# Theta and the mixing over channels in f16 pairs, and the result's addition on GpSimd, in an attention and spectral-mixing kernel

## The chip, the cores and the metric

The kernel runs on one core of a Trainium2 chip. The metric is the device time of one execution in microseconds, the median of several runs. One more execution was recorded by the hardware profiler; all durations below come from it. The engines are TensorE (PE; its weight loads are listed as PEld), VectorE (DVE), ScalarE (ACT), GpSimd (POOL) and SyncE (SP), which here issues the DMAs. L536 is line 536 of the kernel before.

## The reference

Windowed attention (8 batches, 8 heads, 576 positions, heads of 64) gives `x` with 512 channels; then angles, a mixing over positions (tokens), and a mixing over channels:

```python
scores = scale * np.matmul(q, k.transpose(0, 1, 3, 2))
...
scores = np.where(mask, scores + bias[None], -1000000000.0)   # 0 <= rel < 128, slope * -|rel|
attn = np.exp(scores - max); attn = attn / (sum + 1e-09)
x = np.matmul(attn, v)                                        # (8, 576, 512) after the heads are joined
theta = x @ w_theta
zr, zi = x * np.cos(theta), x * np.sin(theta)
y = einsum('ts,bsd->btd', w_tok_r, zr) + einsum('ts,bsd->btd', w_tok_i, zi)
u = x + y
return u + np.maximum(u @ w_ch, 0.0)
```

All inputs but the weights are float32; the weights `w_theta`, `w_tok_r`, `w_tok_i`, `w_ch` arrive as float64 and are turned into float32 values on the chip.

## The kernel before

**Split products.** TensorE multiplies operands of reduced precision, so each product of precise values is made of three: a value is split into a high part and the remainder (`hi`, `lo`), and hi x hi, hi x lo and lo x hi are summed in PSUM. ScalarE writes the high part, VectorE or GpSimd subtracts it from the value for the low one. Two formats are in use. Token mixing (`mix`, L536) and the attention's values (`values`, L424) use float16 pairs; since float16 has a narrow range of exponents, their values are first multiplied by powers of two. Scores (L365), theta (L475) and channel mixing (L557) use pairs in `F32R`, a 32-bit format, with no scaling; the profile lists it as f32. A matmul has a stationary operand of 128 x 128, loaded as weights, and a moving one: 512 columns in theta (the stationary operand is transposed `x`, the moving one `wth`), 288 in token and channel mixing (half of the 576 positions).

**Stages of a batch.** `attend(b + 1)` runs the four pairs of heads of the next batch: scores, biased and exponentiated (`weigh`, L380 and L383), transposed (`flip`, L388, L395, L396), multiplied with the values (L424) and normalised into `x_sb` (`finish`, L430 to L433). Into it is laid the token mixing of batch b: eight groups of 27 matmuls (L536). Each group's sum is scaled back and added to transposed `x` in `xtf` (L541), which is then `u`; ScalarE writes `u_hi` (L543) and GpSimd `u_lo` (L544). Then comes the `turn` of batch b + 1, over five tiles of positions in the order 1, 2, 3, 4, 0 (tile 0 holds only 64 positions, with high and low part in one operand):

- `columns`: four transposes into PSUM (L455); ScalarE copies `x_hi` (L466), VectorE subtracts `x_lo` (L467), ScalarE copies the plain value to `xtf` (L468).
- `products`: 12 theta matmuls (8 for tile 0), L475. The weights of theta carry the factor 1/(2 pi), so theta counts turns.
- `angle`: rounding to whole turns by adding a large constant (`MAGIC`, L489, ScalarE), the remainder (L490, VectorE, which reads theta's PSUM buffer for the last time), its absolute value (L492), cosine and sine (L496, L497, ScalarE), the products with `x` and a scale (L500), and their split (L446 on ScalarE, L447 on GpSimd).

`rotated` lays one of the channel mixing's eight blocks (12 matmuls at L557, then the relu and the addition of `u` in one VectorE instruction, L560, then the store to DRAM, L562) between the tiles of the turn; two blocks come ahead of it, within the attention (`ahead`, `AHEAD`). The last batch has no turn after it: its blocks follow the token mixing.

**Order.** The program is written in an order and with priorities (`urgent`, `MIX`, `CHAN`, `ROTATE`), from which a planner that simulates the time line makes each engine's order of instructions; on the chip each engine takes its instructions in that order. The matmul results of the turn, of both mixings and of the small sums share three PSUM buffers (`ps_m`, tile `mm`), taken in turn.

**Start.** `start` runs the attention of batch 0 while `unpack` brings in the weights: 17 chunks (four of theta, nine of token mixing, then four of channel mixing, `LATE`), each loaded into one of four places, taken apart by VectorE and ScalarE (L149 to L160), multiplied together by GpSimd (L162) and split (`split`, L170). The raw data of the places lie in buffers named `u_hi`, `u_lo` and `xtf`. For token mixing the sum of absolute values of each row gives the row's power of two (`power`, L119). `scales_first` (L279) puts the first batch's scales together after the last chunk: `spread` (L241) brings a maximum over partitions to all of them by a transpose, a small matmul and VectorE instructions. `batch_scale` (L256) makes a batch's scales from the largest values of `v`.

## Time and profile before

| | |
|---|---|
| median of 3 runs | 770.69 us (770.41 to 771.16) |
| the profiled execution | 770.52 us, span 768.7 us |
| TensorE matmul, weight loads | 703.3 us (91% of the span), 579.9 us (75%) |
| VectorE | 570.4 us (74%), 1554 instructions |
| ScalarE | 478.9 us (62%), 948 instructions |
| GpSimd | 215.6 us (28%), 249 instructions |
| channel matmuls (L557) | 3 x 256 of 288 columns |
| theta matmuls (L475) | 160 + 160 + 128 of 512 columns |

The span runs from the first to the last instruction; the profiled execution's own time is longer by what lies around it. The page divides the span into 40 slices of 19.2 us and gives each engine's busy share in tenths. Matmuls are pipelined, so their busy times overlap each other, and a matmul's duration is longer than the distance to the next. In a list of instructions the columns are the start in us, the duration, the engine, the line, the operation, output<-inputs, the shapes and the count; brackets give idle time before it and what ended it. A row of a group gives, behind the bar, busy time and the mean duration in ns, then the idle time ahead of it.

### The profile page before, as it was taken

To read this page: it belongs to the slowest core of one execution; us is meant where nothing else is said; L and a number is where in the kernel's file an instruction comes from. 1 tells how busy PE (TensorE), PEld (TensorE's weight loads), DVE (VectorE), ACT (ScalarE), POOL (GpSimd) and SP (SyncE) were. 2 spreads that over 40 slices of the span, in tenths; PEclk is the share of its full clock that TensorE was granted. 3 is DMA by queue.
4 is the path that set the end of the run, shared out by engine and by line. 5 is a ranking of instruction groups with operands and counts; after the bars stand their busy time and mean duration, and the time that the engine had idled before them with its cause. 6 is when DMAs were issued, how large, how long until landed. Compare 5 with 4: busy or idle time off the path is not lost.

```text
span 768.7 us, 16184 instructions
## 1 busy us (share of the span) xinstructions
PE 703.3 (91%) x6218; PEld 579.9 (75%) x6221; DVE 570.4 (74%) x1554; ACT 478.9 (62%) x948; POOL 215.6 (28%) x249
## 2 busy tenths in 40 slices
PE   3777588999999999989999999999999999999998
PEld 2466476778878887778878887788778887788777
DVE  5999888888579847797579847887579857864722
ACT  3678638856678547774678647774678547844610
POOL 3343524321233105212232204221233105211420
PEclk8678569999999999999999999999999999999999
DMA  7544220312112200321012301321012200100101
GB/s 259 155 154 152 87 65 2 88 46 64 39 55 81 84 32 32 96 55 60 24 55 72 93 32 32 97 68 48 24 55 82 82 32 32 33 2 32 32 1 62
DMA packets 32621, 49.87 MB, mean 65 GB/s; under 512 B 5664, under 2 KB 22048, under 8 KB 32544
## 3 DMA queue, kind: packets, MB, share of 16 engines
q1 hardware_dynamic: 32544, 48.84, 20.8%
q8 instruction: 49, 0.80, 0.4%
q14 instruction: 28, 0.23, 0.1%
HBM read 39.39 MB, written 9.44 MB: 64 GB/s over the span
## 4 chain that ended last, share of the span: by engine, by line
PE 45%; DVE 29%; ACT 15%; DMA 7%; issue 3%; POOL 0%; SPq 0%; DVEq 0%; ACTq 0%; POOLq 0%
PE mm L536 16%; PE mm L557 7%; PE mm L475 6%; DMA vb<-in_vx_dram 5%; PE s_ps L365 5%; PE t_ps L388 5%; PE acc L424 5%; DVE f L490 4%; ACT s_sb L383 3%; DVE g L492 3%; DVE s_sb L380 2%; DVE g L500 2%; ACT f L489 2%; ACT g L496 2%; DVE pt L396 2%
## 5 line engine op out<-in xcount | busy, mean ns | idle before, releaser
L536 PE MATMUL mm<-wtk_hi,z_hi 128*128 128x288 f16 x576 | 161.9, 288 | 6.1 <-DVE f L487 3.6
L536 PE MATMUL mm<-wtk_lo,z_hi 128*128 128x288 f16 x576 | 161.3, 288 | 0.0
L536 PE MATMUL mm<-wtk_hi,z_lo 128*128 128x288 f16 x576 | 158.8, 287 | 0.0
L536 PEld LDWEIGHTS <-z_hi 128*128 128x128 f16 x1152 | 108.9, 98 | 36.3 <-issue 6.7
L383 ACT ACTIVATE s_sb<-s_sb,fixed 128x256 f32<-128x256 f32 (+1 forms) x256 | 102.1, 469 | 16.8 <-DVE fixed L380 16.7
L544 POOL TENSOR_TENSOR u_lo<-xtf,u_hi 128x288 fp32r<-128x288 f32 x64 | 51.8, 816 | 195.1 <-ACT u_hi L543 178.9
L380 DVE CUSTOM_DVE_ANT_0 s_sb<-s_ps,bands 128x256 f32<-128x256 f32 (+1 forms) x256 | 85.1, 383 | 1.3 <-PE s_ps L365 1.3
L396 DVE SCALAR_TENSOR_TENSOR pt<-t_ps,pt 128x512 f16<-128x512 f32 x112 | 75.9, 685 | 10.5 <-ACT pt L395 10.5
L388 PE MATMUL t_ps<-fixed,s_sb 128*128 128x128 f32 x448 | 77.3, 289 | 6.4 <-ACT s_sb L383 2.0
L395 ACT ACTIVATE pt<-t_ps 128x512 f16<-128x512 f32 x112 | 65.2, 588 | 25.0 <-PE t_ps L388 24.4
L447 POOL TENSOR_TENSOR z_lo<-g,z_hi 128x512 f16<-128x512 f32 x32 | 37.7, 1177 | 134.8 <-ACT z_hi L446 134.8
L301 POOL TENSOR_TENSOR kl<-kr,kh 128x576 fp32r<-128x576 f32 x32 | 50.2, 1569 | 64.3 <-ACT kh L300 64.3
L424 PE MATMUL acc<-vh,pt 128*128 128x65 f16 x1008 | 65.7, 195 | 1.9 <-DVE x_sb L433 1.8
L536 PEld LDWEIGHTS <-z_lo 128*128 128x128 f16 x576 | 57.1, 99 | 13.6
L424 PEld LDWEIGHTS <-pt 128*128 128x128 f16 x1512 | 59.8, 98 | 9.8 <-DVE x_sb L433 2.3
L388 PEld LDWEIGHTS t_ps<-fixed,s_sb 128*128 128x128 f32 x448 | 53.6, 148 | 14.5 <-ACT s_sb L383 6.0
L543 ACT CAST u_hi<-xtf 128x288 fp32r<-128x288 f32 x64 | 27.1, 427 | 59.1 <-DVE xtf L541 58.9
L424 PE MATMUL acc<-vl,pt 128*128 128x64 f16 x504 | 56.3, 193 | 0.0
L557 PE MATMUL mm<-u_hi,wch_hi 128*128 128x288 f32 x256 | 53.0, 321 | 1.3 <-DVE xtf L560 1.1
L496 ACT ACTIVATE g<-g,fixed 128x512 f32<-128x512 f32 (+1 forms) x40 | 29.0, 725 | 39.7 <-DVE g L492 39.2
L365 PE MATMUL s_ps<-kh,qh 64*128 64x256 f32 (+1 forms) x256 | 48.9, 344 | 5.1 <-DVE fixed L380 4.5
L475 PE MATMUL mm<-wth_hi,x_hi 128*128 128x512 f32 x160 | 46.0, 409 | 7.9 <-DVE f L490 7.3
(146 smaller groups left out, 1598.4 us busy)
## 6 DMA issues: line engine op xcount, KB each, us to landing
vb<-in_vx_dram SPq DMA_DIRECT2D x16, 650.0 KB, 4.2
kr<-in_kt_dram SPq DMA_DIRECT2D x32, 288.0 KB, 2.9
out_dram<-xtf SPq DMA_DIRECT2D x64, 144.0 KB, 1.8
qr<-in_qt_dram SPq DMA_DIRECT2D x32, 144.0 KB, 2.7
qr<-in_qt_dram SPq DMA_DIRECT2D x32, 128.0 KB, 2.8
xtf<-in_wtok_dram SPq DMA_DIRECT2D x4, 576.0 KB, 5.0
u_hi<-in_wtok_dram SPq DMA_DIRECT2D x3, 576.0 KB, 3.8
u_lo<-in_wtok_dram SPq DMA_DIRECT2D x2, 576.0 KB, 4.4
```

The costliest lines, as they stand in the source:

```text
L301: nc.gpsimd.tensor_tensor(out=kl, in0=kr, in1=kh.bitcast(F32), op=ALU.subtract)
L365: nc.tensor.matmul(ps[:, e, off:off + kn], qm[rows, q0:q0 + qn], km[rows, k0:k0 + kn], start=(j == 0), stop=(j == last))
L380: nc.vector.tensor_tensor_reduce(out=sb, in0=ps, in1=bias, scale=2.0 ** -(2 * self.p % H + 1), scalar=3.0e38, op0=ALU.add, op1=ALU.min, ac ...
L383: self.exp = nc.scalar.activation(sb, sb, AF.Exp, bias=least, scale=-1.0)
L388: nc.tensor.transpose(t_ps[:, 128 * n:128 * n + 128], self.sc[i, e][:, 128 * j:128 * j + 128], ident)
L395: nc.scalar.activation(pt[:, 0], t_ps, AF.Copy, scale=2.0 ** PEXP)
L396: nc.vector.scalar_tensor_tensor(out=pt[:, 1], in0=t_ps, scalar=2.0 ** PEXP, in1=pt[:, 0], op0=ALU.mult, op1=ALU.subtract)
L424: nc.tensor.matmul(av[:, i, :r.shape[-1]], l, r, start=(n == 0), stop=(n == len(prods) - 1))
L475: nc.tensor.matmul(t_ps, a[:, c * 128:c * 128 + 128], w[:, c, :], start=(k == 0 and c == 0), stop=(k == len(prods) - 1 and c == 3))
L536: nc.tensor.matmul(y_ps[:, :HALF], z[:, c, m * 128:m * 128 + 128], w[:, c, cs], start=(k == 0), stop=(k == 26))
L544: nc.gpsimd.tensor_tensor(out=u_lo[:, m, cs], in0=xtf[:, m, cs], in1=u_hi[:, m, cs].bitcast(F32), op=ALU.subtract)
L557: nc.tensor.matmul(o_ps[:, :HALF], w[:, c, e * 128:e * 128 + 128], u[:, c, cs], start=(k == 0), stop=(k == 11))
```

## The change

Theta's and the channel mixing's pairs become float16. All their scales are powers of two: for theta from the largest `v` of the batch and the largest row sum of theta's weights; for the channel mixing from the row sums of its weights and a bound on `u`, for which the column sums of the absolute token weights are formed by 18 matmuls (`absw`). The scales enter as columns of memory: the high part of `x`, the rounding constant, the factors of the sines and the high part of `u` are now ScalarE instructions with such a column as scale or bias. `u_lo` is made by VectorE. The relu scales back on VectorE into a buffer `r`, and `u` is added to it by GpSimd, in the last batch by VectorE. Two of the four raw places get buffers of their own (`stage`). The core of the diff:

```diff
-    wth_hi = const.tile([128, 4, DM], F32R, name="wth_hi")
+    wth_hi = const.tile([128, 4, DM], F16, name="wth_hi")
...  (the same for wth_lo, wch_hi, wch_lo, x_hi, x_lo, u_hi, u_lo)
+            if kind == "theta":
+                nc.gpsimd.tensor_tensor(out=wth_val[:, c, :], in0=val, in1=ex.bitcast(F32), op=ALU.mult)
+                nc.scalar.activation(val, wth_val[:, c, :], AF.Abs, scale=TURN, accum_out=sums[:, c:c + 1])
+                return
             nc.gpsimd.tensor_tensor(out=val, in0=val, in1=ex.bitcast(F32), op=ALU.mult)
...
+            nc.scalar.activation(junk, val, AF.Abs, accum_out=sums[:, 4 + at:5 + at])
+            nc.vector.tensor_scalar(out=sums[:, 4 + at:5 + at], ..., scalar1=2.0 ** -100, scalar2=None, op0=ALU.max)
+            power(rows[:, 1 + at:2 + at], sums[:, 4 + at:5 + at], WEXP)
...
-                nc.scalar.copy(hi[:, c, :], val)
-                nc.gpsimd.tensor_tensor(out=lo[:, c, :], in0=val, in1=hi[:, c, :].bitcast(F32), op=ALU.subtract)
+        def pieces(hi, lo, val, scale):
+            nc.scalar.activation(hi, val, AF.Copy, scale=scale)
+            nc.vector.scalar_tensor_tensor(out=lo, in0=val, scalar=scale, in1=hi, op0=ALU.mult, op1=ALU.subtract)
...
     def scales_first():
...
+        for k in range(2):
+            s_ps = ps_m.tile([128, 512], F32, name="mm")
+            for c in range(9):
+                nc.tensor.matmul(s_ps[:, :HALF], ones..., absw[:, c, k * HALF:k * HALF + HALF], ...)
+            nc.vector.tensor_reduce(out=wide[:, 1 + k:2 + k], in_=s_ps[:, :HALF], ..., op=ALU.max)
...  (some twenty more small VectorE instructions for lim, fac, blim, bfac)
-            nc.scalar.copy(x_hi, x_ps)
-            nc.vector.tensor_tensor(out=x_lo, in0=x_ps, in1=x_hi.bitcast(F32), op=ALU.subtract)
+            nc.scalar.activation(x_hi, x_ps, AF.Copy, scale=xs)
+            nc.vector.scalar_tensor_tensor(out=x_lo, in0=x_ps, scalar=xs, in1=x_hi, op0=ALU.mult, op1=ALU.subtract)
...
-            nc.scalar.activation(r[:n], th, AF.Copy, bias=MAGIC)
+            nc.scalar.activation(r[:n], th, AF.Identity, bias=magic[:n])
...
-                nc.scalar.activation(g[:n], g[:n], AF.Sin, bias=halfpi[:n], scale=-RAD)
-            st["sin"] = nc.scalar.activation(f[:n], f[:n], AF.Sin, scale=-RAD)
+                nc.scalar.activation(g[:n], g[:n], AF.Sin, bias=halfpi[:n], scale=rad[:n])
+            st["sin"] = nc.scalar.activation(f[:n], f[:n], AF.Sin, scale=rad[:n])
...
-                nc.scalar.copy(u_hi[:, m, cs], xtf[:, m, cs])
-                nc.gpsimd.tensor_tensor(out=u_lo[:, m, cs], in0=xtf[:, m, cs], in1=u_hi[:, m, cs].bitcast(F32),
-                                        op=ALU.subtract)
+                us = st["us"][:, m:m + 1]
+                nc.scalar.activation(u_hi[:, m, cs], xtf[:, m, cs], AF.Copy, scale=us)
+                nc.vector.scalar_tensor_tensor(out=u_lo[:, m, cs], in0=xtf[:, m, cs], scalar=us, in1=u_hi[:, m, cs],
+                                               op0=ALU.mult, op1=ALU.subtract)
...
-                nc.vector.scalar_tensor_tensor(out=xtf[:, e, cs], in0=o_ps[:, :HALF], scalar=0.0, in1=xtf[:, e, cs],
-                                               op0=ALU.max, op1=ALU.add)
+                r = rp.tile([128, HALF], F32, name="r")
+                nc.vector.tensor_scalar(out=r, in0=o_ps[:, :HALF], scalar1=st["uback"], scalar2=0.0, op0=ALU.mult,
+                                        op1=ALU.max)
+                (nc.gpsimd if b < B - 1 else nc.vector).tensor_tensor(out=xtf[:, e, cs], in0=r, in1=xtf[:, e, cs],
+                                                                      op=ALU.add)
```

More of the change, by code (lines that the diff above doesn't have):

```diff
@@ L102, in attn_moe_kernel @@
         nc.vector.memset(scales[:, g:g + 1], -0.125 * 2.0 ** (2 * g + 1))
-    wth_hi = const.tile([128, 4, DM], F32R, name="wth_hi")
-    wth_lo = const.tile([128, 4, DM], F32R, name="wth_lo")
-    wch_hi = const.tile([128, 4, DM], F32R, name="wch_hi")
-    wch_lo = const.tile([128, 4, DM], F32R, name="wch_lo")
+    wth_hi = const.tile([128, 4, DM], F16, name="wth_hi")
+    wth_lo = const.tile([128, 4, DM], F16, name="wth_lo")
+    wch_hi = const.tile([128, 4, DM], F16, name="wch_hi")
+    wch_lo = const.tile([128, 4, DM], F16, name="wch_lo")
     wtk_hi = const.tile([128, 9, S], F16, name="wtk_hi")
     wtk_lo = const.tile([128, 9, S], F16, name="wtk_lo")
-    sums, rows, invs, lim = (rings[name].take() for name in ("sum", "row", "inv", "lim"))
+    wth_val = const.tile([128, 4, DM], F32, name="wth_val")
+    absw = const.tile([128, 9, S], BF16, name="absw")
+    sums, rows, invs, back, lim, fac, blim, bfac, wide, rowt = (
+        rings[name].take() for name in ("sum", "row", "inv", "back", "lim", "fac", "blim", "bfac", "wide", "rowt"))
     nc.vector.memset(rebias, -float(916 << 23))
@@ L170, in split @@
[L170 to L184 removed]
+            src, hi, lo, c, w, kind = jobs[k]
@@ new lines, in together, with split @@
+            nc.vector.tensor_scalar(out=sums[:, 4 + at:5 + at], in0=sums[:, 4 + at:5 + at], scalar1=2.0 ** -100,
+                                    scalar2=None, op0=ALU.max)
+            power(rows[:, 1 + at:2 + at], sums[:, 4 + at:5 + at], WEXP)
+        def split(k, t):
+            _, hi, lo, c, w, kind = jobs[k]
+            if kind == "theta":
+                if c < 3:
+                    return
+                nc.vector.tensor_reduce(out=wide[:, :1], in_=sums[:, :4], axis=mybir.AxisListType.X, op=ALU.max)
+                nc.vector.tensor_scalar(out=wide[:, :1], in0=wide[:, :1], scalar1=2.0 ** -100, scalar2=None,
+                                        op0=ALU.max)
+                power(rows[:, :1], wide[:, :1], WEXP)
+                nc.vector.tensor_scalar(out=rowt[:, :1], in0=rows[:, :1], scalar1=TURN, scalar2=None, op0=ALU.mult)
+                for c in range(4):
+                    pieces(hi[:, c, :], lo[:, c, :], wth_val[:, c, :], rowt[:, :1])
+                return
+            at = c if kind == "channel" else 4 + c
+            pieces(hi[:, c, :], lo[:, c, :], words(k, t)[2].bitcast(F32), rows[:, 1 + at:2 + at])
@@ L199, in unpack @@
                 tiles[k] = load(k)
-    JOBS = ([(wth, wth_hi, wth_lo, c, DM, TURN) for c in range(4)]
-            + [(wtok, wtk_hi, wtk_lo, c, S, "row") for c in ORDER])
-    LATE = [(wch, wch_hi, wch_lo, c, DM, None) for c in range(4)]
+    JOBS = ([(wth, wth_hi, wth_lo, c, DM, "theta") for c in range(4)]
+            + [(wtok, wtk_hi, wtk_lo, c, S, "token") for c in ORDER])
+    LATE = [(wch, wch_hi, wch_lo, c, DM, "channel") for c in range(4)]
     def load_pair(p):
@@ L711, in attn_moe_kernel @@
     x_sb = xp.tile([128, NT, DM], F32, name="x_sb")
-    start(x_sb, unpack(JOBS + LATE, ((big, "u_hi"), (big, "u_lo"), (uf, "xtf"), (uf, "xtf"))))
+    start(x_sb, unpack(JOBS + LATE, ((stage, "raw"), (stage, "raw"), (uf, "xtf"), (uf, "xtf"))))
     scales_first()
```

91 lines of the change are left out of this document (49 added, 42 removed).

## The prediction

> **What bounds the kernel now.** I read the page's busy tenths first, then the busy time by stretch, then the order of time on TensorE, then the waits of one stretch.
>
> ```profile
> span 768.7 us, 16184 instructions
> PE   3777588999999999989999999999999999999998
> DVE  5999888888579847797579847887579857864722
> ```
>
> The profiled execution took 770.5 us, 1.8 of them around its span of 768.7; the median of the three runs, 770.69, is 0.2 above it. The sum below is made on 770.5. From the eighth slice (some 135 us) on TensorE is full; before that VectorE is, with nines in slices two to four.
>
> ```profile
> 80.00:98.00 18.00, 8.51 (x46) 7.36 (x46) 14.88 (x46) 9.17 (x19) 8.51 (x6) 0.50 0.26 76
> 98.00:108.00 10.00, 9.30 (x46) 8.43 (x46) 7.57 (x23) 4.22 (x8) 4.00 (x4) 0.50 0.28 79
> 564.50:622.00 57.50, 56.59 (x625) 45.77 (x625) 47.65 (x153) 38.88 (x82) 14.39 (x21) 1.00 0.25 73
> 622.00:650.40 28.40, 26.77 (x160) 23.18 (x159) 17.81 (x33) 17.89 (x32) 8.50 (x8) 1.00 0.08 28
> 564.50:622.00 57.50, 5.55 (x24) 4.05 (x24) 1.00 0.25 73
> 622.00:650.40 28.40, 10.87 (x72) 9.92 (x72) 1.00 0.08 28
> ```
>
> The columns of the first four are TensorE matmul, its weight loads, VectorE, ScalarE, GpSimd, then the granted clock and DMA. The last two rows are the channel matmuls (L557) alone. A steady batch takes 85.9 us: an attention stretch of 57.5, in which the scores of the next batch interleave with the token mixing, and a turn of 28.4 (transposes, theta, angles), into which 72 of the 96 channel matmuls are laid. TensorE is 98% busy in the first and 94% in the second. So a shorter matmul is worth its time in the first stretch, and in the second only where no other chain ends later.
>
> **The matmuls: distance from start to start.** Busy times of matmuls overlap; what counts is the distance between starts.
>
> ```profile
> 406.31 0.29 PE L536 MATMUL mm<-wtk_hi,z_lo 128*128 128x288 f16 x1
> 406.43 0.19 PE L424 MATMUL acc<-vh,pt 128*128 128x65 f16 x1
> ...
> 616.76 0.38 PE L557 MATMUL mm<-u_hi,wch_hi 128*128 128x288 f32 x1
> 616.98 0.20 PE L424 MATMUL acc<-vh,pt 128*128 128x65 f16 x1
> 617.02 0.38 PE L557 MATMUL mm<-u_hi,wch_hi 128*128 128x288 f32 x1
> ...
> 619.47 0.38 PE L557 MATMUL mm<-u_lo,wch_hi 128*128 128x288 f32 x1
> ...
> 623.64 0.69 PE L557 MATMUL mm<-u_hi,wch_lo 128*128 128x288 f32 x4
> 624.16 0.69 PE L557 MATMUL mm<-u_lo,wch_hi 128*128 128x288 f32 x4
> ...
> 626.51 1.07 PE L475 MATMUL mm<-wth_lo,x_hi 128*128 128x512 f32 x4
> 627.42 1.07 PE L475 MATMUL mm<-wth_hi,x_lo 128*128 128x512 f32 x4
> L536 PEld LDWEIGHTS <-z_hi 128*128 128x128 f16 x1152 | 108.9, 98 | 36.3 <-issue 6.7
> L557 PEld LDWEIGHTS mm<-u_hi,wch_hi 128*128 128x128 f32 x256 | 38.8, 190 | 3.4 <-DVE xtf L560 1.7 <-DVE xtf L541 0.4
> ```
>
> An f16 matmul of 288 columns takes 0.12 (406.31 to 406.43), a channel matmul in a block 0.13 (0.52 for four). Alternating with the 65-column matmuls of the values, a channel matmul takes 0.22 and the pair 0.26: the weight load of 190 ns no longer hides under so short a neighbour, one of 98 would. In f16 the pair is 0.12 and 0.04, so 0.10 is saved. Between 616.76 and 619.47 ten channel matmuls stand so.
>
> Term 1, attention stretches: ten at 0.10 and the other 14 at 0.01 give 1.15 each, over seven batches **-8.0**. It rests on the interleaving being the same in the other batches; its bounds are 24 at 0.01 (-1.7 in all) and 24 at 0.10 (-17).
>
> Term 2, turns: 72 channel matmuls at 0.01 are 0.7. A theta matmul of 512 columns takes 0.2275; none in f16 of that size runs here at full clock, so by columns it is 0.12 x 512 / 288 = 0.213, at most 0.014 saved, at the other end nothing. I take the first, as both lengths are streams of columns: 56 make 0.8. Together 1.5 a turn, 12.2 in eight. How much of it counts, the waits say:
>
> ```profile
> PE mm L475 <- DVE f L490: 1.0, 2, 0.5
> 635.75 1.16 POOL L447 TENSOR_TENSOR z_lo<-f,z_hi 128x512 f16<-128x512 f32 x1
> 635.80 1.39 DVE L492 TENSOR_SCALAR g<-f 128x512 int32<-128x512 int32 x1
> 635.82 1.20 PE L475 MATMUL mm<-wth_hi,x_hi 128*128 128x512 f32 x4 [0.53 <-DVE f L490]
> 637.71 0.44 DVE L560 SCALAR_TENSOR_TENSOR xtf<-mm,xtf 128x288 f32<-128x288 f32 x1
> 640.03 0.59 ACT L489 ACTIVATE f<-mm 128x512 f32<-128x512 f32 x1
> ```
>
> In two of a turn's five theta tiles TensorE waits for L490, because theta's PSUM buffer comes free only there: the chain L490, L492, the two sines, L500, the copy to z_hi, L489 is longer than TensorE's work. There shorter matmuls buy only a longer wait. I count three fifths: **-7.3** (bounds 0 and -12.2).
>
> Term 3, after 725 us there is no attention left: 96 channel matmuls of the last batch at 0.01 are -0.95; the result's addition becomes a second VectorE instruction behind the last one, 0.44 by L560, before the last store. Together **-0.5**.
>
> **ScalarE, term 4.** L489, both sines, x_hi and u_hi get their scale or bias as a column of memory instead of a number.
>
> ```profile
> L496 ACT ACTIVATE g<-g,fixed 128x512 f32<-128x512 f32 x32 | 23.2, 725 | 20.3 <-DVE g L492 19.8
> L497 ACT ACTIVATE f<-f 128x512 f32<-128x512 f32 x32 | 19.7, 616 | 0.0
> ```
>
> The cosine with its bias column takes 109 ns more than the sine without. That is 0.11 for L489 and 0.11 for the cosine (its second column; nothing shows one, it could be 0) on the chain of each of the two late tiles; the sine's runs beside L500, and u_hi's and x_hi's on an engine 68% and 63% busy in the two stretches, hidden by that. 2 x 2 x 0.11 x 8 = **+3.5** (half of it to twice it).
>
> **VectorE and GpSimd.** u_lo moves from GpSimd to VectorE; the relu keeps its place (from PSUM, L560's 0.44) and its addition goes to GpSimd for seven batches. x_lo stays: the scaled subtraction from PSUM takes as long as the plain one, 685 ns both.
>
> ```profile
> L544 POOL TENSOR_TENSOR u_lo<-xtf,u_hi 128x288 fp32r<-128x288 f32 x64 | 51.8, 816 | 195.1 <-ACT u_hi L543 178.9 <-PE mm L351 16.2
> L317 DVE SCALAR_TENSOR_TENSOR vl<-vb,fixed,vh 128x320 f16<-128x320 f32 x56 | 30.6, 546 | 0.4 <-ACT vh L315 0.2
> L396 DVE SCALAR_TENSOR_TENSOR pt<-t_ps,pt 128x512 f16<-128x512 f32 x112 | 75.9, 685 | 10.5 <-ACT pt L395 10.5
> L467 DVE TENSOR_TENSOR x_lo<-mm,x_hi 128x512 fp32r<-128x512 f32 x32 | 21.8, 685 | 14.2 <-ACT x_hi L466 14.2
> L541 DVE SCALAR_TENSOR_TENSOR xtf<-mm,fixed,xtf x64: 500/509/518, 149.7 to 758.5; 128x288 f32<-128x288 f32 x64
> L492 DVE TENSOR_SCALAR g<-f x40: 416/518/1399, 115.1 to 728.4; 128x512 int32<-128x512 int32 x32, 64x512 int32<-64x512 int32 x8
> ```
>
> Term 5: by L317, 546 x 288/320 = 0.49 for each u_lo, some seven in an attention stretch: 3.4 more on VectorE, which goes from 47.65 of 57.5 (83%) to 51.1 of 56.4 (91%). Behind u_lo stand the evictions that TensorE's scores wait for. Between 0 and 3.4 a batch; I take 0.2, nearer to nothing because TensorE now loses under 1 us there: **+1.4**.
>
> Term 6: L492, from SBUF to SBUF, takes 416 to 1399 ns, and the 1.39 is from a start 0.05 behind GpSimd's z_lo. L541 with an operand in PSUM keeps within 500 to 518. So GpSimd holds up VectorE's instructions that stay in SBUF. Until now GpSimd's 8.5 us of a turn were z_lo; u_lo ran mostly in the other stretch, and now 72/12 = 6 additions of 0.8 run in the turn. Behind the relu at L560's place come L500, L500 and L492 of the same tile. Bounds: 0, or a whole 0.80 in both late tiles, 1.6 a turn. A third of VectorE's turn (the angles' SBUF instructions) is exposed, so I take a quarter of the upper end: 0.4 a turn, **+3.2**.
>
> The Trainium skill, "SBUF — State Buffer", section on who interferes with whom, says that a VectorE instruction with two SBUF inputs and a GpSimd one that reads SBUF exclude each other for a whole instruction. By that rule both L500 and the new u_lo would be exposed as L492 is, and the term would go to its upper end, +12.8 (a rival below); the trace agrees for L492 at 1399 ns.
>
> **The start.** Each of the four channel weight chunks now takes a row sum, a clamp, two small instructions for its power of two, and a scaled subtraction on VectorE instead of GpSimd; theta's four are split together once their common sum is there; 18 matmuls and some 21 more small VectorE instructions form the scales, which x_hi of the first turn now waits for. The number of loads stays, and so do the queues; two raw buffers move to a pool of their own.
>
> ```profile
> 84.59 0.14 DVE L166 TENSOR_SCALAR fixed<-fixed 128x1 f32<-128x1 f32 x1
> 80.48 0.41 DVE L151 TENSOR_SCALAR xtf<-xtf 128x512 int32<-128x512 int32 x1
> 86.59 1.45 POOL L162 TENSOR_TENSOR xtf<-xtf 128x512 f32<-128x512 f32 x1
> 86.83 1.49 DVE L151 TENSOR_SCALAR xtf<-xtf 128x512 int32<-128x512 int32 x1
> 97.87 0.59 PE L249 MATMUL mm<-fixed 128*128 128x9 f32 x2 [7.25 <-DVE fixed L247]
> ```
>
> Term 7: 33 small ones at 0.14, four subtractions at 0.685 and two maxima at 0.44 are 8.2 us of VectorE between 80 and 108, where it is idle for 3.1 + 2.4 = 5.5. That leaves 2.7 behind; one collision of the L151 kind (1.49 against 0.41) goes with GpSimd's four subtractions. **+2** (from -3, if the values behind L249's wait of 7.25 no longer stand behind it, to +9 with no cover at all). ScalarE's eight sums lie in its idle half (9.17 of 18 busy), the 18 matmuls in TensorE's.
>
> Sum: -8.0 - 7.3 - 0.5 + 3.5 + 1.4 + 3.2 + 2.0 = -5.7, so 764.8, 765 against the median.
>
> **Rivals.** (a) TensorE takes it all: a new order of the angles leaves no tile late, the ScalarE, VectorE and GpSimd terms vanish, terms 1 and 2 count fully: -8.0 - 12.2 - 0.5 + 2.0 gives 752. For it speaks the 98%, against it the two waits of 0.5 in every turn.
> (b) Slower: GpSimd's addition holds L500 or L492 for all its 0.80 in both late tiles, 12.8 instead of 3.2: 774.4. It decides from 1.1 us a turn on. For it L492's 1399, against it that as many of a tile's VectorE instructions read PSUM (L490, L467, the relu) as stay in SBUF (L492, both L500).
> (c) No net change: the start has no cover, +9 instead of +2: 771.8. For it the nines, against it the 5.5 idle.
> That the matmuls do not get shorter at all is excluded at 288 columns by L536, not at 512.
>
> **How the numbers follow.** The forecast has 0.50, (a) 0.18, (b) 0.20, (c) 0.12. The likeliest alone reaches from 759 to 769. With (a) and (b) the range is 752 to 776. 0.2% is 1.5 us, about what a measurement here can tell from nothing. Faster: 0.50 + 0.18 less 0.03 at the edge; same: 0.12 and that edge, less what of (c) is worse; slower: (b) and a little of (c).
>
> **What would show it.** In the trace after: L557 pairs with L424 at 0.16 instead of 0.26 and blocks at 0.12 a matmul (term 1); L475 at 0.213 (term 2); L490's wait on TensorE in a turn, now 1.0, at 2 or more; L489 at 0.70; longest L492 and L500 beside GpSimd's addition (term 6: over 1.1 us a turn is rival b); the first token-mixing matmul of the first batch some 2 us later than now. The prediction is wrong if the planner lays the channel matmuls elsewhere, so that term 1 is gone or doubled, or if the turn's chain gets a different order.

## The result, and the profile after

The changed kernel takes 779.12 us (median of four runs, 777.34 to 781.26) against 770.82 of the kernel before, a ratio of 1.0109 with a 95% interval of 1.0082 to 1.0136. It is slower, by about 8 us; 765 was forecast, with 752 to 776 as the range. The profiled execution took 778.70 us, 776.9 of them its span. Of all executions used below one alone ran in a slower state, the profiled one of the kernel with a constant bound (983 us, at a low clock), and only the order within its start is read. A line number (L514) is that of the kernel which is being read.

The page of the changed kernel: the busy tenths of TensorE and VectorE and the granted clock in 40 slices of 19.4 us. Below it the clock of the kernel before, in slices of 19.2.

```profile
PE   4698669789898999899989999899989998999997
DVE  6998876977877986888688986798688877884844
PEclk9775558999999999999999999999999999999999
```

```profile
PEclk8678569999999999999999999999999999999999
```

The clock row is the first thing to read: it has 5, 5, 5 in the fourth to sixth slices (58 to 117 us), where the kernel before has 8, 5, 6. From the ninth slice on TensorE shows nines and eights, before almost only nines. To find where the time went, three marks are enough: the first theta matmul (end of the start), the first token-mixing matmul of the first batch (end of the first turn) and of the second batch. The summary of one line of code gives its first and last start behind the three durations. First the kernel before, then the changed one:

```profile
L475 PE MATMUL mm<-wth_hi,x_hi x160: 387/393/764, 109.9 to 722.3; 128*128 128x512 f32 x160
L536 PE MATMUL mm<-wtk_hi,z_hi x576: 282/286/448, 130.7 to 756.1; 128*128 128x288 f16 x192
L536 PE MATMUL mm<-wtk_hi,z_hi x1: 283/283/283, 218.8 to 218.8; 128*128 128x288 f16 x1
```

```profile
L514 PE MATMUL mm<-wth_hi,x_hi x160: 376/379/634, 120.4 to 730.1; 128*128 128x512 f16 x160
L575 PE MATMUL mm<-wtk_hi,z_hi x576: 282/286/448, 142.7 to 764.0; 128*128 128x288 f16 x192
L575 PE MATMUL mm<-wtk_hi,z_hi x1: 283/283/283, 235.5 to 235.5; 128*128 128x288 f16 x1
```

| stretch | before | after | difference |
|---|---|---|---|
| start, to the first theta matmul | 109.9 | 120.4 | +10.5 |
| first turn | 20.8 | 22.3 | +1.5 |
| first batch | 88.1 | 92.8 | +4.7 |
| from there to the end of the span | 549.9 | 541.4 | -8.5 |

So all that is lost is lost in the first 235 us, 16.7 us, and the other batches win back half of it. A steady batch of the changed kernel, as busy times by stretch (matmul, weight loads, VectorE, ScalarE, GpSimd, then clock and DMA), and below it the channel matmuls (L597) alone:

```profile
573.70:630.00 56.30, 54.48 (x602) 43.79 (x602) 49.65 (x156) 38.17 (x80) 12.02 (x16) 1.00 0.24 73
630.00:658.20 28.20, 25.11 (x183) 16.27 (x182) 20.16 (x37) 20.56 (x34) 12.84 (x13) 1.00 0.10 33
```

```profile
573.70:630.00 56.30, 3.92 (x24) 2.35 (x24) 1.00 0.24 73
630.00:658.20 28.20, 9.87 (x72) 6.91 (x72) 1.00 0.10 33
```

The attention stretch fell from 57.5 to 56.3, the turn from 28.4 to 28.2; the 24 channel matmuls in the first are busy 3.92 instead of 5.55. The steady part did what it was meant to do. The two stretches hold almost the same work as before, but not quite: in the changed kernel 27 value matmuls of 64 or 65 columns stand in the turn, and five more of token mixing in the attention stretch, so the split between the two is good to some 0.3 us by an estimate; the sum of 84.5 instead of 85.9 does not depend on it.

What happened in the start is read from the chain of work that ended last in the window from 90 to 145 us of the changed kernel (start, duration, engine, what it writes, line):

```profile
92.85 4.16 DMA raw<-in_wch_dram
...
100.63 4.07 PE acc L461 x18
104.70 0.23 PE mm L259
...
105.34 1.36 DVE peak L252
...
106.89 0.60 PE mm L265 x2
107.50 4.34 PE mm L306 x18
...
111.86 0.46 DVE fixed L308
...
113.42 0.81 PE mm L388 x3
```

This is one thread through three engines. The last channel chunk lands at 97.0; it is unpacked and split; the last value matmuls follow at 100.6, for 4.07 at half clock; then the maxima are transposed (L259), reduced (L261), spread over the partitions (L265), the weights' row sums are added on TensorE (L306, 4.34 us) and reduced (L308), and only at 113.3 does TensorE take up the scores of the next batch, 8.7 us after L259. No engine is full in it: from 104.7 to 113.4 TensorE is busy for 5.9 us and VectorE for 6.6. In the kernel before, the scales of the first batch take nothing from the channel chunks and are spread at 97.9, ahead of the last value matmuls, behind which the next scores (L351) come at once:

```profile
99.02 4.07 PE L424 MATMUL acc<-vb,pt 128*128 128x65 f32 x18
102.89 0.53 PE L249 MATMUL mm<-fixed 128*128 128x4 f32 x2
103.28 0.51 PE L351 MATMUL mm<-kh,qh 128*128 128x192 f32 x1
```

From the start of these value matmuls to the next scores it takes 4.3 us before and 12.7 after. These 8.4 are the larger part of the start's 10.5; 1.6 more had come ahead of them, where the last chunk lands 2.5 us later (94.5 before).

TensorE between 100 and 130 us, first before, then after:

```profile
100.00:110.00 10.00, 9.39 (x49) 8.65 (x48) 7.61 (x20) 4.17 (x9) 2.74 (x3) 0.50 0.43 125
110.00:120.00 10.00, 10.00 (x60) 8.43 (x59) 6.54 (x19) 7.75 (x14) 0.10 (x1) 0.97 0.01 3
120.00:130.00 10.00, 8.06 (x62) 6.49 (x61) 9.81 (x23) 7.78 (x16) 4.77 (x5) 1.00 0.00 1
```

```profile
100.00:110.00 10.00, 7.39 (x33) 6.15 (x34) 5.85 (x16) 1.44 (x3) 1.03 (x2) 0.50 0.22 67
110.00:120.00 10.00, 8.28 (x41) 6.58 (x40) 9.02 (x44) 4.61 (x9) 1.44 (x1) 0.50 0.21 59
120.00:130.00 10.00, 10.00 (x57) 5.49 (x56) 4.13 (x10) 5.94 (x10) 0.00 (x0) 0.84 0.02 4
```

Busy time by clock gives TensorE's work at full speed: 9.39 x 0.50 + 10.00 x 0.97 + 8.06 = 22.5 us before, 7.39 x 0.50 + 8.28 x 0.50 + 10.00 x 0.84 = 16.2 after. In these 30 us 6.2 are lost, and the larger part of them by the clock. TensorE's idle time in these rows grew from 2.6 to 4.3, but what it lost by running busy below full speed grew from 5.0 to 9.4: before, the row of 110 to 120 has a clock of 0.97, after the next one still has 0.84. In rows of one us the clock comes to full between 110 and 111 us before, between 123 and 124 after.

### The profile page after: what moved, and what is told of

It reads as the page before. It is cut to its first block, busy times and chain, and to the rows that moved or that the text cites. A ratio compares the mean times of both kernels' runs of the same rounds, so it can differ in the third digit from the quotient of the medians.

```text
span 776.9 us, 16320 instructions
## 1 busy us (share of the span) xinstructions
PE 695.1 (89%) x6236; PEld 520.1 (67%) x6239; DVE 615.4 (79%) x1668; ACT 500.9 (64%) x964; POOL 216.5 (28%) x237
## 3 DMA queue, kind: packets, MB, share of 16 engines
q1 hardware_dynamic: 32544, 48.84, 20.3%
## 4 chain that ended last, share of the span: by engine, by line
PE 49%; DVE 26%; ACT 16%; issue 4%; DMA 4%; POOL 1%; SPq 0%; DVEq 0%; ACTq 0%; POOLq 0%
PE mm L575 20%; PE acc L461 6%; PE t_ps L425 6%; PE s_ps L402 6%; PE mm L597 5%; DVE f L529 4%; DVE g L531 3%; ACT g L535 3%; PE mm L514 3%; ACT s_sb L420 3%; DVE g L539 2%; ACT f L528 2%; DVE ql L335 2%; DVE x_lo L506 1%; DVE s_sb L417 1%
## 5 line engine op out<-in xcount | busy, mean ns | idle before, releaser
L575 PE MATMUL mm<-wtk_hi,z_hi 128*128 128x288 f16 x576 | 164.7, 289 | 12.3 <-DVE f L526 9.1
L420 ACT ACTIVATE s_sb<-s_sb,fixed 128x256 f32<-128x256 f32 (+1 forms) x256 | 103.7, 470 | 25.9 <-DVE fixed L417 25.2
L603 POOL TENSOR_TENSOR xtf<-r,xtf 128x288 f32<-128x288 f32 x56 | 56.0, 1000 | 104.9 <-DVE r L601 104.9
L432 ACT ACTIVATE pt<-t_ps 128x512 f16<-128x512 f32 x112 | 63.0, 586 | 24.0 <-PE acc L461 19.4
L338 POOL TENSOR_TENSOR kl<-kr,kh 128x576 fp32r<-128x576 f32 x32 | 47.2, 1475 | 108.1 <-ACT kh L337 80.9
L583 ACT ACTIVATE u_hi<-xtf,fixed 128x288 f16<-128x288 f32 x64 | 33.1, 531 | 67.0 <-DVE xtf L580 66.4
L575 PEld LDWEIGHTS <-z_lo 128*128 128x128 f16 x576 | 57.1, 99 | 14.4
L535 ACT ACTIVATE g<-g,fixed 128x512 f32<-128x512 f32 (+1 forms) x40 | 32.6, 814 | 46.9 <-DVE g L531 46.7
L514 PEld LDWEIGHTS <-x_hi 128*128 128x128 f16 x320 | 31.4, 99 | 46.4 <-issue 16.9
L461 PE MATMUL acc<-vh,pt 128*128 128x65 f16 x1008 | 61.3, 194 | 0.0
L425 PEld LDWEIGHTS t_ps<-fixed,s_sb 128*128 128x128 f32 x448 | 52.7, 148 | 12.7 <-ACT s_sb L420 7.7
L353 POOL MEMSET vh<- 128x5 f16 x56 | 6.7, 120 | 194.0 <-PE acc L461 145.0
L461 PEld LDWEIGHTS <-pt 128*128 128x128 f16 x1512 | 57.1, 98 | 4.6 <-DVE pt L433 0.2
L597 PEld LDWEIGHTS <-wch_hi 128*128 128x128 f16 x512 | 49.2, 98 | 14.6 <-issue 1.1
L461 PE MATMUL acc<-vl,pt 128*128 128x64 f16 x504 | 55.4, 193 | 0.0
```

Source lines behind the costliest of these rows:

```text
L338: nc.gpsimd.tensor_tensor(out=kl, in0=kr, in1=kh.bitcast(F32), op=ALU.subtract)
L420: self.exp = nc.scalar.activation(sb, sb, AF.Exp, bias=least, scale=-1.0)
L425: nc.tensor.transpose(t_ps[:, 128 * n:128 * n + 128], self.sc[i, e][:, 128 * j:128 * j + 128], ident)
L432: nc.scalar.activation(pt[:, 0], t_ps, AF.Copy, scale=2.0 ** PEXP)
L461: nc.tensor.matmul(av[:, i, :r.shape[-1]], l, r, start=(n == 0), stop=(n == len(prods) - 1))
L514: nc.tensor.matmul(t_ps, a[:, c * 128:c * 128 + 128], w[:, c, :], start=(k == 0 and c == 0), stop=(k == len(prods) - 1 and c == 3))
```

## The experiments

Theory T1 was that the start is a serial chain that the new scales make longer; its rival T2 that the steady work (additions on GpSimd, columns of memory) costs the time and the start's delay is made up later. Each kernel was timed beside the kernel before; the ratios are to that.

**The bound on u as a constant.**

```diff
-        for k in range(2):  ... 18 matmuls over absw, two maxima, two small instructions
+        nc.vector.memset(wide[:, 3:], 64.0)
```

> The 18 matmuls that sum |weights| by row, their two maxima and the small instructions behind them are left out; the bound on u is the constant 64 instead (the bound's computation is left out). T1, the start: in the changed kernel these lie on the chain to the first turn, 106.9 to about 113 us, with TensorE at half clock, so the first token-mixing matmul comes 4 to 6 us earlier than at 142.7 and the whole takes some 774 (779 less 5). T2, the steady work: the additions on GpSimd and the memory columns cost the time, the start's delay is made up later: within 1 us of the changed kernel, 778 to 779.

778.27 us, ratio 1.0083 (1.0051 to 1.0114): some 2 us less than the changed kernel's 1.0109, with intervals that overlap; 4 to 6 was expected. The chain of this kernel tells why; from 80 us to the first theta matmul its clock is 0.50, as in the changed kernel:

```profile
102.11 4.07 PE acc L453 x18
...
106.21 4.11 DMA vb<-in_vx_dram
...
110.34 1.49 DVE peak L252
```

With the 18 matmuls gone, another wait ends last. VectorE takes its instructions in order, and the maximum of the next values (L252), which needs a load, stands in the middle of the scale's small instructions. Counted from the start of the value matmuls it ends 9.7 us behind them, the 18 matmuls of the changed kernel 11.2, so only 1.5 us are won there. The first theta matmul comes at 118.8, 1.6 earlier; the first token mixing, for which 4 to 6 was expected, can't be read from this execution. The 18 matmuls lay on the chain with their whole 4.34 us, but there was another chain right under them.

**The channel scale behind the first turn.**

```diff
-    scales_first(): maxima of v, theta, token and channel spread together, 18 matmuls, 15 factors
+    scales_first(): the same for v, theta and token alone, 11 factors
...
     rotated(turn(x_sb, st[0]), iter(()))
+    scales_channel()          # channel maximum, 18 matmuls, the other 4 factors
```

> The scales of v, theta and the token weights are formed first and x_hi of the first turn waits only for them; the channel weights' scale, with its 18 matmuls and small instructions, comes behind the first turn. The channel chunks are still unpacked in the start. T1: the first turn loses the wait for the last channel chunk and the chain behind it, the first token-mixing matmul comes 6 to 9 us earlier, the whole takes 770 to 773. T2: no gain over 1 us, 778 to 779.

766.0 us, ratio 0.9936 (0.9915 to 0.9958): not only the loss is gone, the kernel is faster than before. That is more than was expected. Its three marks, and its row of 100 to 130 us in tens:

```profile
L542 PE MATMUL mm<-wth_hi,x_hi x160: 376/379/634, 111.4 to 717.9; 128*128 128x512 f16 x160
L603 PE MATMUL mm<-wtk_hi,z_hi x576: 282/286/397, 137.3 to 751.7; 128*128 128x288 f16 x192
L603 PE MATMUL mm<-wtk_hi,z_hi x1: 283/283/283, 222.4 to 222.4; 128*128 128x288 f16 x1
```

```profile
100.00:110.00 10.00, 9.02 (x45) 8.31 (x46) 8.35 (x34) 5.25 (x10) 2.42 (x3) 0.50 0.35 102
110.00:120.00 10.00, 10.00 (x58) 6.03 (x57) 6.00 (x18) 5.54 (x9) 0.00 (x0) 0.79 0.10 28
120.00:130.00 10.00, 8.78 (x65) 4.85 (x64) 9.18 (x22) 8.74 (x17) 4.96 (x5) 1.00 0.00 0
```

The first theta matmul is back at 111.4, 9.0 earlier and 1.5 behind the kernel before; TensorE does 21.2 us of work in these 30, 5.0 of the 6.2 that were lost. The first turn gets longer (25.9 instead of 22.3, since the scale is now formed in it), the first batch shorter (85.1 instead of 92.8). So of the 12.0 us lost up to the first token mixing 5.4 come back, and 7.7 more in the first batch, which no term and no theory had foreseen; it is taken up below. This settles T1 against T2: the same work, elsewhere, is worth 13 us, and the steady batches had been shorter already.

**The unpacking of the channel weights, too.**

```diff
-    start(x_sb, unpack(JOBS + LATE, ...))
+    start(x_sb, unpack(JOBS, ...))
...
+    late = unpack(LATE, ((stage, "raw"), (stage, "raw")))
-    rotated(turn(x_sb, st[0]), iter(()))
+    rotated(turn(x_sb, st[0]), late)
```

> As the kernel with the channel scale behind the first turn, and the unpacking of the channel weights too is laid into the first turn instead of the start. T1: the start is then no longer than in the kernel before but for theta's joint split, so the first token-mixing matmul comes at 130 to 133 instead of 142.7 and the whole takes 766 to 769; the first turn itself may get 1 to 3 us longer from the unpacking. T2: within 1 us of the changed kernel, 778 to 779.

769.7 us, ratio 0.9992 (0.9978 to 1.0005), 3.7 more than without this step. The first theta matmul stays at 112.2, so the unpacking itself did not hold up the start; it made the first turn 2.7 longer (first token mixing at 140.8, not 130 to 133). What the start lost was the scale's chain, not the weights' throughput.

**The result's addition on VectorE.**

```diff
-                (nc.gpsimd if b < B - 1 else nc.vector).tensor_tensor(out=xtf..., in0=r, in1=xtf..., op=ALU.add)
+                nc.vector.tensor_tensor(out=xtf..., in0=r, in1=xtf..., op=ALU.add)
```

> The addition of u to the result stays on VectorE in all batches; nothing else differs from the changed kernel. T1: GpSimd's hold on VectorE and 0.45 more per addition on VectorE about cancel, the time stays within 2 us of the changed kernel, 777 to 781. T2: GpSimd's additions cost at least the predicted 0.4 a turn, so 3 to 8 us are won, 771 to 776, and the contended L531 and L539 of a turn (up to 1.27 and 1.64) fall back to 0.42 and 0.75.

778.18 us, ratio 1.0098 (1.0078 to 1.0118): the same as the changed kernel, as T1 had it. A steady batch of it, and one of the instructions that GpSimd was to hold up, first in the changed kernel, then here (shortest/median/longest):

```profile
574.10:630.10 56.00, 54.45 (x603) 43.80 (x603) 50.04 (x158) 38.06 (x80) 9.43 (x13) 1.00 0.25 73
630.10:658.20 28.10, 25.02 (x182) 16.21 (x180) 21.99 (x43) 20.39 (x34) 7.40 (x8) 1.00 0.10 32
```

```profile
L539 DVE SCALAR_TENSOR_TENSOR f<-x_sb,fixed,f x32: 742/746/1287, 130.2 to 733.3; 128x512 f32<-128x512 f32 x32
```

```profile
L539 DVE SCALAR_TENSOR_TENSOR f<-x_sb,fixed,f x32: 737/744/747, 129.1 to 733.1; 128x512 f32<-128x512 f32 x32
```

A steady batch is 0.4 shorter (84.1 for 84.5; 0.3 on the average of the five behind the first), although VectorE then does 2.2 us more in it. The second L539 of a tile is no longer held (747 at most, 1287 with the addition on GpSimd). The first L539 still is, up to 1.64, and L531 up to 1.38, with no addition on GpSimd; its z_lo remains. So the addition on GpSimd costs 0.3 to 0.4 a batch more than a second instruction on VectorE would. That is near the size of term 6, but 0.3 of it fall in the attention stretch (56.3 to 56.0) and 0.1 in the turn, where term 6 had placed it. In this kernel the first batch (95.5) ate it.

**The channel scale inside the first token mixing.**

```diff
-    scales_channel()                      # behind the first turn
+                    if st["b"] == 0 and hf == 0 and m == 0 and k == 9:
+                        scales_channel()  # inside mix()
```

> As the kernel with the channel scale behind the first turn (766.0, first token-mixing matmul at 137.3), but the channel scale is formed a little later, inside the token mixing of the first batch, ahead of the first u_hi. If the instructions of that scale (18 matmuls, some 20 small VectorE instructions) hold up the end of the first turn, where VectorE is full and TensorE waits, the first token-mixing matmul comes 2 to 4 us earlier, at 133 to 135, the first batch stays at some 85, and the whole takes 762 to 764. Rival: VectorE has the same work ahead of it wherever it stands; then the first batch gets longer by what the turn gets shorter, 765.5 to 766.5.

770.01 us, ratio 0.9989 (0.9973 to 1.0005), 4 more than behind the first turn. The first token mixing did come at 133.7, 3.6 earlier, and the first batch then took 93.7 instead of 85.1. The rival had the direction and missed the size.

**The same with the addition on VectorE.** Its edit is the last one and that of the addition together.

> As the kernel with the channel scale inside the first token mixing, and the result's addition on VectorE in all batches. With the steady batches at 84.2 instead of 84.5 as in the changed kernel with that addition, 1.5 to 2 us less than the kernel it starts from. Rival: with the start repaired VectorE is the fuller engine in the first batch, and the addition costs there what it wins later: no difference over 0.7 us.

767.17 us, ratio 0.9955 (0.9938 to 0.9972): 2.8 less, a little more than the steady batches give (84.1 to 84.5 us in its profile, 84.4 to 85.9 in that of the kernel it starts from).

**The angles with numbers instead of columns.**

```diff
-            nc.scalar.activation(r[:n], th, AF.Identity, bias=magic[:n])
+            nc.scalar.activation(r[:n], th, AF.Copy, bias=MAGIC)
-            ... scalar=magic[:n] ...            (L529's subtraction)
+            ... scalar=MAGIC ...
-                ... AF.Sin, bias=halfpi[:n], scale=rad[:n])      (and the sine)
+                ... AF.Sin, bias=halfpi[:n], scale=-1e-20)
```

> As the kernel with the channel scale behind the first turn (766.0), with the angle's scale and bias given as numbers in the instructions instead of columns of memory (wrong numbers: the scaling of the angles is left out). By term 4 each of the two late tiles of a turn wins 0.22: 3.5 us less, 762 to 763, with the turn of a steady batch 0.4 shorter. Rival: TensorE or VectorE bound these places anyway: 765.3 to 766.3.

775.19 us, ratio 1.006 (1.0037 to 1.0083): 9 more than the kernel it starts from, against both expectations. The single instructions did get shorter, as ScalarE's groups show (mean behind the busy time; here the cosine), first of the kernel that this one starts from, then of this one:

```profile
L563 ACT ACTIVATE g<-g,fixed 128x512 f32<-128x512 f32 (+1 forms) x40 | 32.6, 814 | 45.3 <-DVE g L559 45.2
```

```profile
L563 ACT ACTIVATE g<-g,fixed 128x512 f32<-128x512 f32 (+1 forms) x40 | 28.9, 723 | 53.7 <-DVE g L559 53.6
```

A column costs 91 ns at the cosine (814 less 723), and 89 at L556, the eviction (681 less 592). The Trainium skill, "ScalarE: Activation LUTs", section "What ACT_TABLE_LOAD costs", gives about 93 ns for each such operand; the trace agrees. But the planner that sets the order of every queue reacts to such an edit as well: the order of TensorE's instructions differs in many places, and a steady batch takes 85.6 instead of 84.4. What term 4 alone is worth can't be told from this kernel and stays open.

**Theta alone.**

```diff
-    wch_hi, wch_lo, u_hi, u_lo in F16, with the channel scale and its bound
+    the same in F32R as before; u_lo on GpSimd; relu and addition in one VectorE instruction
```

> Only theta takes f16 pairs; the channel mixing is as in the kernel before (32-bit floats, u_lo on GpSimd, relu and addition in one VectorE instruction), and its bound and scale are left out. By the chain theory the start is then that of the kernel before but for theta's joint split: first token-mixing matmul at 131 to 135. By terms 1 and 2 the attention stretch goes back to 57.5 and the turn to 28 to 28.4, so a steady batch takes 85.5 to 86: 768 to 771 in all. Rival: the steady gain comes from the turn and not from the channel matmuls: a steady batch stays at 84.5, 762 to 765 in all.

769.91 us, ratio 1.0001 (0.9981 to 1.002). The first theta matmul comes at 111.4 and the first token mixing at 130.8: almost no loss in the start (109.9 and 130.7 before). A steady batch:

```profile
565.20:622.30 57.10, 56.41 (x623) 45.79 (x623) 47.56 (x151) 39.18 (x83) 14.68 (x21) 1.00 0.25 72
622.30:650.10 27.80, 25.70 (x162) 18.57 (x160) 17.84 (x34) 18.98 (x31) 8.16 (x8) 1.00 0.09 32
```

84.9: theta's half of the change wins 0.4 in the attention stretch and 0.6 in the turn; the channel's half wins another 0.8 in the first (57.1 to 56.3) and gives back 0.4 in the second (27.8 to 28.2). With the addition on VectorE that stretch still takes 28.1, so the addition on GpSimd is not the larger part of the 0.4. The forecast of 85.5 to 86 for this batch was too high, the rival's 84.5 nearer. What it wins in the later batches it loses in the first, which takes 94.1, although no channel scale holds up its start.

**No channel scale at all.**

```diff
     def scales_channel():
-        ... maximum, 18 matmuls, powers
+        for t in (lim[:, 11:15], fac[:, 11:15], blim[:, 2:3], bfac[:, 2:3]):
+            nc.vector.memset(t, 1.0)
```

> As the kernel with the channel scale behind the first turn (766.0), with that scale left out: its transpose, broadcast, 18 matmuls, maxima and powers are replaced by constants (the scaling of u is left out); the channel chunks are unpacked in the start as before. If what is left of the loss (second batch's first token-mixing matmul at 222.4 against 218.8 in the kernel before) is the channel scale's own work in the first turn, that point comes at 218.5 to 220 and the whole takes 762 to 763.5. Rival: it is theta's scale and the unpacking; then 221.5 to 222.5 and 765 to 766.

769.67 us, ratio 0.9991 (0.997 to 1.0013), slower than with the scale formed behind the first turn. The first token mixing came at 131.9: without the channel scale 10.8 of the 12.0 us lost up to there come back. But the first batch took 94.2. Neither expectation allowed for that: the time that the first batch loses here does not come from the scale's work.

**Matmuls that nothing reads, in the idle stretches of the start.**

```diff
+                if new is None:
+                    fill(12)
                 one.values()
...
+                if new is None:
+                    fill(10)
                 two.values()
...
         nc.tensor.transpose(m_ps[:, :128], peak, ident)     # in spread()
+        if n > 4:
+            fill(4)
```

> The changed kernel with 30 matmuls more that nothing reads, 512 columns each, laid ahead of the value products of the last pair of the start (12 and 10) and between the two steps that spread a maximum over the partitions (4, twice), where TensorE waited (80.9 to 86.4, 95.9 to 100.6, 104.9 to 106.9, 112.1 to 112.8). If the half clock through 95 to 123 comes from those idle stretches, the clock there is 1.00, the 18 value matmuls at 100.6 take 2.6 instead of 4.07, the 18 of the bound 2.2 instead of 4.34, and the first turn starts at full clock: 3 to 7 us less, 772 to 776. Rival: the clock does not depend on them, or the chain on VectorE bounds this stretch anyway: 778 to 781.

772.73 us, ratio 1.0032 (1.0011 to 1.0053), 6 less than the changed kernel: work was added and time was won. It was 26 matmuls and not 30, since only the first spreading got its four. The 22 of the last pair were ordered earlier than meant, ahead of 78 us, and L259 comes hardly earlier by them (104.34, in the changed kernel 104.49). The four stand in the gap behind L259 (three are in the trace). These, and the row of 100 to 130 us in tens:

```profile
104.98 1.49 PE L614 MATMUL mm<-bands,fixed 128*128 128x512 bf16 x3 [0.22 <-issue]
```

```profile
100.00:110.00 10.00, 9.03 (x36) 6.71 (x38) 5.85 (x17) 1.44 (x3) 0.97 (x2) 0.50 0.22 67
110.00:120.00 10.00, 7.16 (x46) 4.95 (x45) 9.81 (x48) 5.96 (x11) 1.44 (x1) 0.84 0.22 63
120.00:130.00 10.00, 10.00 (x75) 5.92 (x73) 5.26 (x10) 6.72 (x11) 0.00 (x0) 0.96 0.00 1
```

From L259 to the first theta matmuls TensorE's order is that of the changed kernel but for the filling, which bridges a gap of 2 us ahead of the 18 matmuls. The clock comes to full between 110 and 111 us instead of between 123 and 124 (0.84 instead of 0.50 in the 110 to 120 row); with the filling itself counted TensorE does 20.1 us of work in the 30 for 16.2. The first theta matmul comes at 118.3 instead of 120.4. So some 2 us of the start's loss were the idle TensorE's clock and not the chain's length. The rest of the 6 comes behind that point, 2.0 of it in the first turn (20.3), where the order differs too, and is not separated.

**Later scale with the addition on VectorE; with the filling; with both.** No new edit: `scales_channel()` behind the first turn, with `nc.vector` for the addition, with the three `fill` lines, and with both. First the addition:

> The kernel with the channel scale behind the first turn (766.0) and the result's addition on VectorE in all batches. By the steady batches of the kernel that differs in that addition alone (84.2 for 84.5) and the 2.8 that it won with the scale inside the mixing: 1.5 to 2.8 less, 763 to 764.5. Rival: its first batch, which is the shortest of all with 85.1, has no room for the addition on VectorE: 766 to 768.

763.89 us, ratio 0.9918 (0.9886 to 0.995), 2.1 less than with the addition on GpSimd, as expected.

Then the filling:

> The kernel with the channel scale behind the first turn (766.0) and the same matmuls that nothing reads in the last pair of the start and in the spreading of the maxima. If the clock is what is left of the start's loss (13.4 us at half clock from 80 to 137 in that kernel): 3 to 5 us less, 761 to 763. Rival: VectorE bounds this start, which is busy through 92 to 106 without a gap over 0.7: 765.5 to 767.

765.17 us, ratio 0.9937 (0.9912 to 0.9962), no more than the same kernel without the filling (0.9936), as the rival had it, though in the profile every mark from the first theta matmul on (109.7) comes 1.7 to 1.8 us earlier. The rival's reason is not shown: from 92 to 106 VectorE is busy for 10.9 of the 14 us in this kernel, for 13.1 in the one without the filling.

Then both:

> The two edits that won together: channel scale behind the first turn with the result's addition on VectorE (763.9), and the matmuls that nothing reads in the start (765.2 against 766.0 without them). If they add, the first theta matmul comes near 110, steady batches take 84.2, and the whole 762 to 763.5. Rival: the filling matmuls only won by chance of order: 763.5 to 765.

762.91 us, ratio 0.9909 (0.9883 to 0.9935), the fastest of all, though from the 0.9918 without the filling it can't be told apart. Both kernels of the case are beaten by it.

**The first batch.** In most of these kernels the first batch takes 92 to 95 us, in those with the channel scale right behind the first turn about 85 (87.6 with numbers in the angles), but their first turn is at least 3 us longer. The two together, from the first theta matmul to the token mixing of the second batch, take 108.9 us before, 115.1 in the changed kernel, 111.0 with the scale behind the first turn, 114.0 with no channel scale and 113.4 with theta alone. The last two form no channel scale and lose 4.5 to 5 us here all the same, so the late chain is not what they lose it by. The 22.3 us behind the first token-mixing matmul, in the kernel before, the changed one, the one with the scale behind the first turn, and the one with no channel scale:

```profile
130.70:153.00 22.30, 21.30 (x206) 16.42 (x206) 20.06 (x57) 19.52 (x41) 9.88 (x10) 0.92 0.24 64
142.70:165.00 22.30, 18.91 (x145) 12.99 (x144) 15.59 (x41) 17.84 (x35) 8.20 (x7) 0.85 0.10 27
137.30:159.60 22.30, 21.05 (x212) 16.85 (x211) 20.39 (x64) 17.32 (x36) 4.63 (x5) 0.98 0.30 85
131.90:154.20 22.30, 17.20 (x140) 12.42 (x140) 15.11 (x44) 17.16 (x35) 7.83 (x6) 0.85 0.10 27
```

With the scale behind the first turn the token mixing starts later, and then TensorE is idle for 1.3 us at a clock of 0.98; with no channel scale it starts 5.4 us earlier and is idle for 5.1 at 0.85. VectorE stands still in the changed kernel from 158 to 163, and for 5.5 us in the one with no channel scale. In the changed kernel this instruction ends the wait:

```profile
163.20 0.22 DVE L467 TENSOR_SCALAR fixed<-acc,fixed 128x5 f32<-128x5 f32 x1 [5.12 <-PE acc L461]
```

TensorE is busy with token mixing meanwhile, at first with 0.24 us from start to start (158.25 to 158.49) and later with 0.12, and the value matmuls (L461) that VectorE waits for stand behind it.

```diff
-MIX, MIX0, CHAN, CHAN0, ROTATE = -100, 0, -60, -300, 100
+MIX, MIX0, CHAN, CHAN0, ROTATE = -100, -100, -60, -300, 100
```

> The changed kernel with one number different: the token mixing of the first batch gets the same low priority behind the next batch's attention as in the other batches (-100 instead of 0). If the first batch is long (92.8 against 88.1 before and 84.5 later) because token-mixing matmuls stand ahead of the next scores in TensorE's order while VectorE waits for those (it is idle at 159 to 163), the first batch falls to 85 to 88 and the whole to 771 to 775. Rival: the order there is set by the late scale chain and the clock (half through 155 to 161), not by the priority: 92 to 93 and 778 to 780.

774.96 us, ratio 1.0064 (1.0042 to 1.0086): 2.4 of the first batch are gone (90.4), of 5 to 8 expected. But they did not come from the place that the expectation names: VectorE still waits there for 5.2 us, behind the same token-mixing matmuls. Where the 2.4 come from is not shown, and why a token mixing that starts later makes the first batch so much shorter (137.3 and 85.1 against 131.9 and 94.2) is not settled.

## Why the prediction was wrong

- **Term 7, the start, is the step that failed:** +2 (at most +9) was forecast, +12.0 measured to the first token mixing and +16.7 with the first batch. The term was made as a sum of VectorE's work (8.2 us) against VectorE's idle time (5.5), and the 18 matmuls were put at nothing, as lying in TensorE's idle half. But in the row from 98 us on TensorE was busy for 9.30 of 10, and in the changed kernel they stand in its order behind the spreading and ahead of the next scores, where they took 4.34. The prediction itself said that x_hi of the first turn waits for all scales, but it did not follow that wait: the last chunk's arrival, its split, the transpose, the spreading, the matmuls and the powers stand one behind the other, so idle time of an engine elsewhere covers none of it. The runs show it: with the same scale behind the first turn 9.0 of the 10.5 up to the first theta matmul come back, and with no channel scale 10.8 of the 12.0 up to the first token mixing.
- **The clock was left out of term 7.** The quoted row of 98 to 108 us had 0.50 in it. With the longer chain and its gaps TensorE stays at that clock for some 12 us more, and a token-mixing matmul, to take one, takes 0.24 at it instead of 0.12. The filling shows that some 2 us of the loss up to the first theta matmul were this.
- **The first batch (+4.7) was in no term.** It is not the start's delay going on: the two kernels without a channel scale reach the first token mixing nearly as early as the kernel before (131.9 and 130.8) and lose 6 us in this batch (94.2 and 94.1). So it shows with theta's half of the change alone. The traces show TensorE idle and at a lower clock in it, and the priority of its token mixing is worth 2.4; its cause stays open.
- **Terms 1 and 5 hold in size.** The attention stretch was forecast at -0.95 a batch (1.15 less 0.2); it fell by 1.2, 0.8 of them from the channel's half. u_lo took 0.51 (0.49 forecast). But term 1 counted on ten channel matmuls that alternate with value matmuls; in the changed kernel one of the 24 stands beside one (before, 11 did), and the others lie in blocks of four or between token-mixing matmuls. The prediction had named such a new order as a way to be wrong, so that the size came out near is in part luck.
- **Terms 2, 4 and 6 together** were forecast at -0.08 a turn, and the turn fell by 0.2. Theta matmuls are 379 ns in the trace instead of 393 (0.014 forecast); TensorE's wait for L529 grew from 1.0 to 1.4 and that for L526 from 0.6 at the longest to 1.5, so the gain went into waits, more of it than the two fifths that term 2 took off. Term 6, as far as the kernel with the addition on VectorE shows it, was 0.3 to 0.4 a batch, and most of that outside the turn. Term 4's price of one column was 0.09, not 0.11; its effect on the time was not isolated. Columns on VectorE were priced at nothing and cost some 60 ns each: x_lo takes 745 ns instead of 684, L529 748 instead of 689, the relu 510 instead of 450 (medians); "685 ns both" did not hold for x_lo. And terms 2 and 6 count eight turns, though the first turn has no channel matmuls and no additions; the two errors, 0.4 us each, cancel.
- **Term 3:** from the last batch's token mixing on the span takes 44.2 us instead of 43.5: +0.7, not -0.5.
- **The rivals:** (b), GpSimd's additions, gave the right sign for the wrong reason. The second L539 of a tile is held by the addition as it said, but L531 and the first L539 are held without it too (up to 1.38 and 1.64), and the turn fell all the same. u_lo, which the prediction saw exposed as well, was never held (0.52 at the longest), in a stretch where GpSimd is busy for 12.0 of 56.3 us; and L492, at which it sees its rule for two inputs in SBUF agree, has only one. (c) had the right place: the start with "no cover at all", +9. It was closer than the forecast, yet it too counted only VectorE's work, and called the whole no net change.

The waits of TensorE in a steady batch of the changed kernel, in total, times and longest:

```profile
PE mm L575 <- DVE f L526: 3.0, 2, 1.5
PE mm L514 <- DVE f L529: 1.4, 1, 1.4
```

## What to carry to other kernels

Where an edit adds a value that the next stage waits for, don't weigh its instructions against an engine's idle time: write the chain from the last input to the first user, with every engine that it crosses, in the order of each queue, and at the clock that the profile shows there. Then ask who needs the value first; here the channel scale was needed a whole turn later than it was formed, and moving it turned a loss of 1.1% into a gain of 0.6%, and with the addition back on VectorE 0.8%. Taking away the longest link of such a chain wins only up to the next chain that runs beside it. And judge an edit by the whole time, not by the mark that it was made for: the kernel with no channel scale reaches the first token mixing 5.4 us earlier than the one with the scale behind the first turn, and takes 3.7 us longer in all.

## What was not expected of the hardware

- Adding matmuls that nothing reads made the changed kernel 6 us faster; some 2 of them came through the clock ahead of the first theta matmul.
- TensorE can be busy without a gap and still at half clock. In the changed kernel:

```profile
87.00:96.00 9.00, 9.00 (x47) 8.62 (x46) 7.76 (x35) 6.98 (x17) 1.65 (x2) 0.50 0.18 56
```

The Trainium skill, "TensorE: Matmul & The Clock Gate", section "What's actually happening", has full speed come after some 3.4 us of sustained work. Here 9 us of recorded busy time, mostly 65-column value matmuls and some scores, all in 32-bit floats, did not bring it, so the trace does not agree. Perhaps less counts as work for the clock than the trace records as busy; no run here tests that.
